# Norm factors of four batches: from scaled identities and products with ones to a store in DRAM and a broadcast read

## The chip, the cores and the metric

The kernel runs on one core of a Trainium2 chip. The metric is the device time of one execution in microseconds, the median of several. The engines are TensorE (PE, with its weight loads PEld), VectorE (DVE), ScalarE (ACT), GpSimd (POOL) and SyncE (SP, which here only issues DMAs). Each engine runs its own instructions in order.

## What is computed

Three layers follow each other on 4 x 576 = 2304 tokens of 512 features: a retention (attention with decaying causal weights, 8 heads), a gated unit behind an RMS norm, and a mixture of 8 experts with Sinkhorn-normalised weights. The change touches the norm at the start of the gated unit:

```python
rms = np.sqrt(np.mean(x * x, axis=-1, keepdims=True) + 1e-06)
xn = x / rms * rms_g
g = xn @ w_gate
silu = g * (1.0 / (1.0 + np.exp(-g)))
val = xn @ w_val
return (silu * val @ w_out).astype(np.float32)
```

`x` is the retention's output. 1/rms is one factor per token.

## The kernel before

Features lie on the 128 partitions, tokens in the free dimension: `acc_d[:, pr, tokens]` holds 128 of the 512 features. The program is written in the order in which each engine shall run it (a manual schedule); no planner moves anything.

**Retention.** 16 pairs of heads, pair i = batch b times 4 plus pr. In step i of the loop the code issues loads for pairs i+2 (q and v) and i+3 (k, twice), the scores of pair i+1 (`scores`, tile `sc`, then on VectorE the product with the mask, `am`), the states of pair i+1 (`states`), and the outputs of pair i (`outputs`, tile `o`, PSUM; VectorE multiplies it into `acc`, line 345). ScalarE squares the result (`sq`), GpSimd adds the squares of a batch's four pairs (line 352). `step_weights` puts one step of the preparation of the gated unit's weights (tiles `raw`, `cv`, `wslots`) into each pair. A pair's q has three buffers, k has two; all loads but the first are issued by SyncE, each when its buffer is free.

**The norm** of batch b is two generators that the loops push on, one step at a time.

- `norm_sums(b)`: products of the squares with ones put the tokens on the partitions (`ss`), a power of -0.5 on GpSimd (`ry`), and one pair later a Newton step on VectorE. The result `r` is 128 x 5: token c*128 + p lies at partition p, column c.
- `norm(b)`: the factors have to stand along the free dimension on all partitions. ScalarE scales an identity by each column of `r` (tile `dg`), TensorE multiplies it with ones (`rb`, `rbt`), ScalarE copies the result to `y`. Then follow four steps, one for each `pr`: VectorE scales `x` by `y` and the weight `rms_g` in place, ScalarE rounds it to `xhi`, and VectorE or GpSimd takes the rest, `xlo`, of the step before.

`SUMS_AT` places the sums of batches 0 to 2 at pairs 5 and 6, 9 and 10, 13 and 14; batch 3's follow in the first block of the gated unit. `norm(0)` starts with pair 7 and makes one step in each pair; `norm(1)` makes its first two steps in pairs 13 and 15:

```python
if i >= 2 * NP - 1:
    next(norms[0], None)
if i in (B * NP - 3, B * NP - 1):
    next(norms[1])
```

**The gated unit** runs over 5 blocks of tokens. A block multiplies its tokens with two gate and two value slices (`gv`, four times 12 products), forms the gated product (`t`, then `ghi` and `glo`), and multiplies it with two slices of the output weight (`x`). The first block begins when the retention has ended, and its first PSUM tile takes the bank of the last `o`. The norm of batch j+1 is made within block j.

Of the kernel before, what the change touches and what calls it, by code (L numbers as in the profile page):

```python
# [9 lines left out]
F32 = mybir.dt.float32  # L10
# [7 lines left out]
B, H, S, D = 4, 8, 576, 64  # L18
NP = H // 2
# [6 lines left out]
C = 128  # L26
NC = S // C
TAIL = S - NC * C
# [23 lines left out]
def retention_glu_experts(ctx: ExitStack, tc: tile.TileContext, a, out):  # L52
# [6 lines left out]
    nc = tc.nc  # L59
# [6 lines left out]
    kept = ctx.enter_context(tc.tile_pool(name="kept", bufs=1, space=bass.MemoryType.DRAM))  # L66
# [6 lines left out]
    ident = const.tile([128, 128], F32, name="ident")  # L73
    ones = const.tile([128, 128], F32, name="ones")
# [9 lines left out]
    def f32(t):  # L84
        return t.bitcast(F32)
# [13 lines left out]
    nrm = glu.enter_context(tc.tile_pool(name="nrm", bufs=1, side="right"))  # L99
# [3 lines left out]
    def load_weights(most=2):  # L103
        for _ in range(most):
            if n_load[0] == len(sources) or not raw_slots:
                return
            i = n_load[0]
            n = raw_of[i] = raw_slots.pop(0)
            t = rawp.tile([128, 1024], I32, tag=f"raw{n}", name=f"raw{i}")
            nc.sync.dma_start(t, sources[i].bitcast(I32))  # L110
            raw[i], asked[i] = t, n_step[0]
            n_load[0] += 1
# [37 lines left out]
    def step_weights(load=True, apart=2):  # L150
        for i in sorted(active):
            if next(active[i], True):
                del active[i]
        i = n_next[0]
        n_step[0] += 1
        if i in raw and len(active) < NCONV and n_step[0] - asked[i] > apart:
            active[i] = prepare(i)
            next(active[i])
            n_next[0] += 1
        if load:  # L160
            load_weights()
# [81 lines left out]
    psa = psa_pools.enter_context(tc.tile_pool(name="psa", bufs=2, space=PSUM))  # L243
# [15 lines left out]
    def load_pair(i, *names, queue=nc.sync):  # L259
        if i >= B * NP:  # L260
            return
        b, pr = divmod(i, NP)
        t = {}
        for n in names:
            t[n] = ld.tile([128, a[n].shape[-1]], F32, tag=n, name=f"{n}{i}", bufs=2 if n[0] == "k" else 3)
            queue.dma_start(t[n], a[n][b, pr])
        loaded.setdefault(i, {}).update(t)

    def scale_keys(i):
        if i >= B * NP:  # L270
            return
        for h in range(2):
            hh = 2 * (i % NP) + h
            ks = loaded[i]["ks"].rearrange("p (c h d) -> p c h d", h=2, d=D)[:, :, h, :]
            nc.scalar.mul(ks, ks, g_key[:, hh:hh + 1])
# [77 lines left out]
        squares[b] = sq  # L353
        yield

    normed, rstd = set(), {}

    def bank(name):
        pool, tag = ps_home
        return pool.tile([128, 512], F32, tag=tag, name=name)  # L360

    def two_banks(b):
        if b < 2:
            t = psa.tile([128, 2, 512], F32, tag="sc", name=f"rb{b}")
            return t[:, 0], t[:, 1]
        return bank(f"rb{b}"), bank(f"rbt{b}")

    def norm_sums(b):

        sq = squares.pop(b)  # L370
        if b < B - 1:
            ss = psa.tile([128, 2, 512], F32, tag="sc", name=f"ss{b}")[:, 0, :NC + 1]
        else:
            ss = bank(f"ss{b}")[:, :NC + 1]
        for c in range(NC + 1):
            w = C if c < NC else TAIL
            nc.tensor.matmul(ss[:w, c:c + 1], lhsT=sq[:, c * C:c * C + w], rhs=ones[:, :1], start=True, stop=True)
        v = nrm.tile([128, NC + 1], F32, tag="rv", name=f"rv{b}")
        r = nrm.tile([128, NC + 1], F32, tag=f"ry{b}", name=f"ry{b}")
        t = nrm.tile([128, NC + 1], F32, tag="rt", name=f"rt{b}")  # L380
        nc.vector.memset(v, 1.0)
        nc.vector.tensor_scalar(v[:, :NC], ss[:, :NC], 1.0 / DM, 1e-6, ALU.mult, ALU.add)
        nc.vector.tensor_scalar(v[:TAIL, NC:], ss[:TAIL, NC:NC + 1], 1.0 / DM, 1e-6, ALU.mult, ALU.add)
        nc.gpsimd.tensor_tensor(out=r, in0=v, in1=mhalf, op=ALU.pow)
        yield
        nc.vector.tensor_mul(t, r, r)
        nc.vector.scalar_tensor_tensor(t, t, -0.5, v, ALU.mult, ALU.mult)
        nc.vector.scalar_tensor_tensor(r, t, 1.5, r, ALU.add, ALU.mult)
        rstd[b] = r

    def norm(b):
        r = rstd.pop(b)
        dg = nrm.tile([128, (NC + 1) * C], F32, tag="dg", name=f"dg{b}")
        dg = dg.rearrange("p (c i) -> p c i", i=C)
        for c in range(NC + 1):
            nc.scalar.mul(dg[:, c, :], ident, r[:, c:c + 1])
        yield
        rb, rt = two_banks(b)
        rt = rt[:, :TAIL]
        nc.tensor.matmul(rb, lhsT=ones, rhs=dg[:, :NC, :], start=True, stop=True)  # L400
        nc.tensor.matmul(rt, lhsT=ones[:TAIL, :], rhs=dg[:TAIL, NC, :TAIL], start=True, stop=True)
        y = nrm.tile([128, (NC + 1) * C], F32, tag="dg", name=f"y{b}")[:, :S]
        nc.scalar.copy(y[:, :NC * C], rb)
        nc.scalar.copy(y[:, NC * C:], rt)
        yield
        ts = slice(b * S, (b + 1) * S)
        for pr in range(NP):
            x = acc_d[:, pr, ts]
            nc.vector.scalar_tensor_tensor(x, x, rms_g[:, pr:pr + 1], y, ALU.mult, ALU.mult)
            nc.scalar.copy(xhi[:, pr, ts], x)  # L410
            if pr:
                p = acc_d[:, pr - 1, ts], f32(xhi[:, pr - 1, ts])
                (nc.vector if pr % 2 else nc.gpsimd).tensor_sub(xlo[:, pr - 1, ts], *p)
            yield
        nc.vector.tensor_sub(xlo[:, pr, ts], acc_d[:, pr, ts], f32(xhi[:, pr, ts]))
        normed.add(b)

    ps_home = [psa, "o"]
    sums, norms = [norm_sums(b) for b in range(B)], [norm(b) for b in range(B)]
# [34 lines left out]
    for i in range(B * NP):  # L454
        b, pr = divmod(i, NP)
        load_pair(i + 2, "qT", "vs")
        load_weights(1)
        if i == 2:
            nc.sync.dma_start(rms_g, a["rms_g"])
            nc.sync.dma_start(ident, a["ident"])  # L460
            nc.sync.dma_start(wg[:, :KD * E], a["wg"])
        scores(i + 1)
        states(i + 1)
        load_pair(i + 3, "kT", "ks")
        scale_keys(i + 2)
        out_steps = outputs(i)
        next(out_steps)
        step_weights(load=False, apart=1)
        next(out_steps)
        if i in SUMS_AT:  # L470
            next(sums[i // NP - 1], None)
        if i >= 2 * NP - 1:
            next(norms[0], None)
        if i in (B * NP - 3, B * NP - 1):
            next(norms[1])
    assert 0 in normed
    retention.close()
# [145 lines left out]
    for s in range(NSWEEP):  # L623
        last_sweep = s == NSWEEP - 1
        for j, (t0, n) in enumerate(BLOCKS):
            last = j == len(BLOCKS) - 1
            block = gated_block(s, t0, n, last, pmm, pac, hp, tp, 1 if last_sweep and last else KD, 512)
            first_norms = not s and j + 1 < B
            assert s or (t0 + n - 1) // S in normed
            for i in range(2 * SWEEP + 1):  # L630
                if last_sweep and last and i == 2 * SWEEP:
                    break
                if first_norms and j and not i:
                    next(norms[j + 1])
                if i == 2 * SWEEP:
                    step_weights()
                next(block)
                if first_norms:
                    for _ in range((1, 1, 1, 2, 0)[i]):
                        next(norms[j + 1], None)  # L640
                    if not j and i in (1, 2):
                        next(sums[B - 1], None)
                    if i == 2 * SWEEP - 1 and j + 2 < B:
                        next(norms[j + 2])
                if i == 2 * SWEEP or i < 2 and not first_norms or i == 2 and not s:
                    step_weights()
                if last_sweep and j and i % 2:
                    next(scored)
                if last_sweep and j == 1 and i == 2:
                    load_job(0)  # L650
                    load_job2(0)
                if last_sweep and j >= 3:
                    next(first_unit, None)
                    if j == 4:
                        next(first_job, None)
            else:
                for _ in block:
                    assert 0
# [648 lines left out]
```

## Time and profile before

| | |
|---|---|
| median of 3 runs | 2000.43 us (1999.23 to 2001.38) |
| the profiled execution | 1999.34 us, its span 1997.6 us |
| TensorE busy | 1980.8 us, 99% of the span |
| VectorE, ScalarE, GpSimd busy | 72%, 44%, 37% |
| granted TensorE clock | 1.000 on average (2.4 GHz) |
| DMA | 436.56 MB, mean 219 GB/s |
| retention | about the first 85 us |

The page gives the busy time of each engine and a chain of waits. How the parts of the first 125 us hang together is read from the timelines of the engines: start, length, engine, line, operation, tiles, and in brackets for how long the engine had been idle and what ended that. A timeline merges equal instructions that follow each other ("x16").

### The profile page before, as it was taken

What the parts mean: (1) busy time and instruction counts of PE and PEld (TensorE: products, weight loads), DVE (VectorE), ACT (ScalarE), POOL (GpSimd) and SP (SyncE); (2) the same over time, 40 slices, a digit from 0 to 9 for tenths busy, and PEclk for the clock granted to TensorE, in tenths of its full rate; (3) what the DMA queues carried; (4) which work ended last, traced back from release to release, by engine and by line L of the source; (5) the groups of instructions that cost most, each with busy time, mean ns of one, the idle gap of its engine ahead of it and who ended that gap; (6) DMA issues with size and microseconds to landing.
All of it is one profiled execution on the core that took longest, in us unless ns stands there. A gap on an engine that the chain in (4) does not pass through costs nothing.

```text
span 1997.6 us, 29892 instructions
## 1 busy us (share of the span) xinstructions
PE 1980.8 (99%) x11390; PEld 1854.0 (93%) x11390; DVE 1442.0 (72%) x2275; ACT 869.0 (44%) x1649; POOL 744.1 (37%) x693
## 2 busy tenths in 40 slices
PE   9999999999999999999999999999999999999998
PEld 7788988988888999999999999999999999999998
DVE  7865555554688777777786777777787777777777
ACT  4453323322454544444444444444445444444443
POOL 3300000000154445455534544445466454444543
PEclk9999999999999999999999999999999999999999
DMA  9411111110188888888888676767767677676763
GB/s 318 147 32 53 53 42 53 43 43 1 48 308 304 289 296 309 306 299 308 299 314 314 247 277 237 278 247 270 262 241 282 258 262 275 239 267 248 275 257 143
DMA packets 111535, 436.56 MB, mean 219 GB/s; under 512 B 11720, under 2 KB 29128, under 8 KB 95008
## 3 DMA queue, kind: packets, MB, share of 16 engines
q1 hardware_dynamic: 109904, 432.39, 59.2%
q8 instruction: 89, 1.46, 0.3%
q10 hardware_dynamic: 1248, 1.49, 0.2%
q0 software_dynamic: 240, 0.79, 0.1%
q14 instruction: 54, 0.44, 0.1%
HBM read 312.41 MB, written 122.21 MB: 218 GB/s over the span
## 4 chain that ended last, share of the span: by engine, by line
PE 95%; DVE 3%; ACT 1%; DMA 1%; POOL 0%; issue 0%; ACTq 0%; DVEq 0%
PE pz L747 10%; PE py L747 10%; PE px L747 10%; PE qx L992 7%; PE qy L992 6%; PE qz L992 6%; PE gv L178 5%; PE gv L180 5%; PE gv L179 5%; PE y L179 4%; PE y L180 4%; PE y L178 4%; PE qz L747 3%; PE x L179 2%; PE x L178 2%; PE x L180 2%
## 5 line engine op out<-in xcount | busy, mean ns | idle before, releaser
L747 PE MATMUL py<-sx,w1s 128*128 128x384 f32 x1152 | 232.0, 336 | 0.8 <-ACT py L1084 0.6
L539 POOL TENSOR_TENSOR t<-rw 128x256 f32<-128x256 f32 x32 | 43.8, 1369 | 503.7 <-DVE sx L576 397.2
L1173 POOL TENSOR_TENSOR acc<-z,a_block 128x384 f32<-128x384 f32 x63 | 64.0, 1016 | 434.6 <-DVE z L1167 434.6
L747 PEld LDWEIGHTS py<-sx,w1s 128*128 128x128 f32 x1152 | 203.0, 188 | 4.9 <-ACT py L1084 1.9
L747 PE MATMUL px<-xhi,w1s 128*128 128x384 f32 x640 | 188.8, 335 | 1.0 <-DVE t L206 1.0
L982 ACT CAST xhi<-acc 128x384 fp32r<-128x384 f32 x316 | 156.0, 514 | 69.7 <-POOL acc L1173 35.5
L986 DVE TENSOR_TENSOR xlo<-acc,xhi 128x384 fp32r<-128x384 f32 x191 | 178.5, 961 | 1.8 <-ACT xhi L982 1.8
L986 POOL TENSOR_TENSOR xlo<-acc,xhi 128x384 fp32r<-128x384 f32 x125 | 148.6, 1189 | 26.3 <-ACT xhi L982 26.3
L1000 DVE TENSOR_TENSOR acc<-acc,qz 128x384 f32<-128x384 f32 x246 | 134.9, 548 | 25.2 <-PE qz L992 25.1
L206 DVE TENSOR_TENSOR t<-t,gv 128x512 f32<-128x512 f32 (+1 forms) x60 | 38.0, 634 | 123.5 <-PE gv L180 122.3
L747 PEld LDWEIGHTS px<-xhi,w1s 128*128 128x128 f32 x640 | 117.9, 188 | 1.5 <-DVE t L206 1.3
L1000 DVE TENSOR_TENSOR acc<-acc,qx 128x384 f32<-128x384 f32 x123 | 67.4, 548 | 71.2 <-PE qx L992 71.2
L747 PE MATMUL pz<-sx,w1s 128*128 128x384 f32 x576 | 115.4, 334 | 0.0
L747 PE MATMUL pz<-xhi,w1s 128*128 128x384 f32 x384 | 113.9, 337 | 0.8 <-DVE z L915 0.8
L792 DVE SCALAR_TENSOR_TENSOR acc<-y,prob,acc 128x512 f32<-128x512 f32 x144 | 101.4, 742 | 8.2 <-PE y L180 8.2
L747 PE MATMUL px<-xlo,w1s 128*128 128x384 f32 x320 | 107.0, 334 | 0.0
L1018 ACT COPY qz<-qy 128x384 f32<-128x384 f32 x127 | 58.8, 463 | 106.8 <-PE qy L992 101.0
L180 PE MATMUL y<-xlo,xhi 128*128 128x512 f32 x264 | 103.8, 393 | 0.0
L179 PE MATMUL y<-xlo,xhi 128*128 128x512 f32 x264 | 103.6, 393 | 0.0
L178 PE MATMUL y<-xlo,xhi 128*128 128x512 f32 x264 | 102.6, 389 | 0.0
L747 PEld LDWEIGHTS pz<-sx,w1s 128*128 128x128 f32 x576 | 101.3, 188 | 0.7
L1010 ACT COPY qy<-qx 128x384 f32<-128x384 f32 x127 | 58.8, 463 | 95.2 <-PE qx L992 89.4
(397 smaller groups left out, 5880.5 us busy)
## 6 DMA issues: line engine op xcount, KB each, us to landing
w1s<-w_kept SPq DMA_DIRECT2D x64, 1792.0 KB, 7.1
w_kept<-w1s SPq DMA_DIRECT2D x32, 1792.0 KB, 6.6
rw<-in_w_dram SPq DMA_DIRECT2D x64, 512.0 KB, 5.4
w_kept<-xlo SPq DMA_DIRECT2D x64, 512.0 KB, 3.7
w2s<-w_kept SPq DMA_DIRECT2D x32, 1024.0 KB, 6.9
w_extra<-w_kept SPq DMA_DIRECT2D x32, 768.0 KB, 7.5
w_kept<-xlo SPq DMA_DIRECT2D x44, 384.0 KB, 4.2
w2c<-w_kept SPq DMA_DIRECT2D x32, 512.0 KB, 7.8
```

Source lines behind the costliest of these rows:

```text
L178: nc.tensor.matmul(ps, lhsT=lh, rhs=rh, start=start, stop=False)
L179: nc.tensor.matmul(ps, lhsT=lh, rhs=rl, start=False, stop=False)
L180: nc.tensor.matmul(ps, lhsT=ll, rhs=rh, start=False, stop=stop)
L747: nc.tensor.matmul(ps, lhsT=l, rhs=r[:, k, :], start=start and k == 0 and i == 0, stop=k == 1 and i == 2, skip_group_check=True,)
L792: nc.vector.scalar_tensor_tensor(o, y_2, pe, o, ALU.mult, ALU.add)
L982: nc.scalar.copy(hi, x)
L986: (engine or nc.vector).tensor_sub(lo, x, f32(hi))
L992: nc.tensor.matmul(ps, lhsT=l, rhs=r, start=start and i == 0, stop=i == 2, skip_group_check=True)
L1000: nc.vector.tensor_add(dst, dst, ps)
L1010: nc.scalar.copy(y, x)
L1018: nc.scalar.copy(z, y)
L1173: nc.gpsimd.tensor_add(sums[0], z[:, 0, :], h_blocks[0])
```

## The change

`norm_sums` ends with a store of `r` to DRAM, written so that the 576 tokens of a batch lie one behind the other there. `norm` begins with a load that reads this row for all 128 partitions into `y`. Scaled identities, products with ones and copies, and the PSUM tiles for them (`two_banks`), are gone. `norm(0)` now starts with pair 9 (the load) and scales in pairs 10 to 13; before, it scaled in pairs 9 to 12. `norm(1)` makes its first step (the load) in pair 14, and its four scalings one step of block 0 later. Both new DMAs are issued by SyncE.

```diff
@@ -386,22 +382,11 @@
         nc.vector.tensor_mul(t, r, r)
         nc.vector.scalar_tensor_tensor(t, t, -0.5, v, ALU.mult, ALU.mult)
         nc.vector.scalar_tensor_tensor(r, t, 1.5, r, ALU.add, ALU.mult)
-        rstd[b] = r
+        nc.sync.dma_start(rstd_kept[b].rearrange("c p -> p c"), r)
 
     def norm(b):
-        r = rstd.pop(b)
-        dg = nrm.tile([128, (NC + 1) * C], F32, tag="dg", name=f"dg{b}")
-        dg = dg.rearrange("p (c i) -> p c i", i=C)
-        for c in range(NC + 1):
-            nc.scalar.mul(dg[:, c, :], ident, r[:, c:c + 1])
-        yield
-        rb, rt = two_banks(b)
-        rt = rt[:, :TAIL]
-        nc.tensor.matmul(rb, lhsT=ones, rhs=dg[:, :NC, :], start=True, stop=True)
-        nc.tensor.matmul(rt, lhsT=ones[:TAIL, :], rhs=dg[:TAIL, NC, :TAIL], start=True, stop=True)
-        y = nrm.tile([128, (NC + 1) * C], F32, tag="dg", name=f"y{b}")[:, :S]
-        nc.scalar.copy(y[:, :NC * C], rb)
-        nc.scalar.copy(y[:, NC * C:], rt)
+        y = nrm.tile([128, S], F32, tag="y", name=f"y{b}")
+        nc.sync.dma_start(y, rstd_kept[b].rearrange("c p -> (c p)")[:S].partition_broadcast(128))
         yield
         ts = slice(b * S, (b + 1) * S)
         for pr in range(NP):
@@ -469,9 +454,9 @@
         next(out_steps)
         if i in SUMS_AT:
             next(sums[i // NP - 1], None)
-        if i >= 2 * NP - 1:
+        if i >= 2 * NP + 1:
             next(norms[0], None)
-        if i in (B * NP - 3, B * NP - 1):
+        if i == B * NP - 2:
             next(norms[1])
     assert 0 in normed
     retention.close()
@@ -630,13 +615,11 @@
             for i in range(2 * SWEEP + 1):
                 if last_sweep and last and i == 2 * SWEEP:
                     break
-                if first_norms and j and not i:
-                    next(norms[j + 1])
                 if i == 2 * SWEEP:
                     step_weights()
                 next(block)
                 if first_norms:
-                    for _ in range((1, 1, 1, 2, 0)[i]):
+                    for _ in range(((1, 1, 1, 2, 0) if j else (0, 1, 1, 2, 1))[i]):
                         next(norms[j + 1], None)
                     if not j and i in (1, 2):
                         next(sums[B - 1], None)
```

Not shown: `two_banks` and the table `rstd` are removed, and `rstd_kept`, four DRAM tiles of 5 x 128, is added. On TensorE and ScalarE the change only takes instructions away or, for the rounding to `xhi`, puts them one pair or step later. On SyncE and VectorE it moves others past them. In the rows below a name's last number is the tile's number in its build.

SyncE, loads around the end of pair 6 and the start of pair 7. Before, the loads of k and q for pair 9:

```order
L266 DMA kT_618<-in_kT_dram 128x576
L266 DMA ks_620<-in_ks_dram 128x512
L266 DMA qT_654<-in_qT_dram 128x576
L266 DMA vs_656<-in_vs_dram 128x576
L266 DMA kT_683<-in_kT_dram 128x576
L266 DMA ks_685<-in_ks_dram 128x512
```

And now:

```order
L266 DMA kT_622<-in_kT_dram 128x576
L266 DMA ks_624<-in_ks_dram 128x512
L385 DMA rstd_kept_117<-ry_585 128x5x1
L266 DMA qT_659<-in_qT_dram 128x576
L266 DMA vs_661<-in_vs_dram 128x576
L266 DMA kT_688<-in_kT_dram 128x576
L266 DMA ks_690<-in_ks_dram 128x512
```

The store of batch 0's factors now stands ahead of q and v of pair 9. In the same way batch 1's store stands ahead of q and v of pair 13, behind k of pair 13; the loads of y stand behind k of pair 12 (batch 0) and behind batch 2's store (batch 1).

VectorE, from the output product of pair 10 to the mask product of pair 12 (`rt`, `ry` are the Newton step of batch 1). Before:

```order
L345 TENSOR_TENSOR acc<-o_906,g_out 128x512
L386 TENSOR_TENSOR rt_862<-ry_861 128x5
L387 SCALAR_TENSOR_TENSOR rt_862<-rt_862,rv_860 128x5
L388 SCALAR_TENSOR_TENSOR ry_861<-rt_862,ry_861 128x5
L409 SCALAR_TENSOR_TENSOR acc<-acc,rms_g,y_789 128x576
L413 TENSOR_TENSOR xlo<-acc,xhi 128x576
L294 TENSOR_TENSOR am_947<-sc_946,masks 128x1024
```

And now:

```order
L345 TENSOR_TENSOR acc<-o_899,g_out 128x512
L382 TENSOR_TENSOR rt_855<-ry_854 128x5
L383 SCALAR_TENSOR_TENSOR rt_855<-rt_855,rv_853 128x5
L384 SCALAR_TENSOR_TENSOR ry_854<-rt_855,ry_854 128x5
L394 SCALAR_TENSOR_TENSOR acc<-acc,rms_g,y_860 128x576
L294 TENSOR_TENSOR am_940<-sc_939,masks 128x1024
```

The first `xlo` has left this place; it stands one pair later, behind one scaling.

VectorE, from the norm's part in pair 13 to the end of pair 14 (`rt`, `ry`: batch 2). Before:

```order
L415 TENSOR_TENSOR xlo<-acc,xhi 128x576
L294 TENSOR_TENSOR am_1153<-sc_1152,masks 128x1024
L314 SCALAR_TENSOR_TENSOR block_states_116<-acc,u_1151 128x256
L315 SCALAR_TENSOR_TENSOR mt_1173<-u_1151,tables 128x64
L343 TENSOR_TENSOR acc<-u_1076,g_out 128x64
L133 SCALAR_TENSOR_TENSOR cv_997<-raw_873,cv_997 128x512
L345 TENSOR_TENSOR acc<-o_1176,g_out 128x512
L386 TENSOR_TENSOR rt_1139<-ry_1138 128x5
L387 SCALAR_TENSOR_TENSOR rt_1139<-rt_1139,rv_1137 128x5
L388 SCALAR_TENSOR_TENSOR ry_1138<-rt_1139,ry_1138 128x5
L343 TENSOR_TENSOR acc<-u_1151,g_out 128x64
```

And now:

```order
L394 SCALAR_TENSOR_TENSOR acc<-acc,rms_g,y_860 128x576
L398 TENSOR_TENSOR xlo<-acc,xhi 128x576
L294 TENSOR_TENSOR am_1142<-sc_1141,masks 128x1024
L314 SCALAR_TENSOR_TENSOR block_states_116<-acc,u_1140 128x256
L315 SCALAR_TENSOR_TENSOR mt_1162<-u_1140,tables 128x64
L343 TENSOR_TENSOR acc<-u_1069,g_out 128x64
L133 SCALAR_TENSOR_TENSOR cv_990<-raw_866,cv_990 128x512
L345 TENSOR_TENSOR acc<-o_1165,g_out 128x512
L382 TENSOR_TENSOR rt_1132<-ry_1131 128x5
L383 SCALAR_TENSOR_TENSOR rt_1132<-rt_1132,rv_1130 128x5
L384 SCALAR_TENSOR_TENSOR ry_1131<-rt_1132,ry_1131 128x5
L400 TENSOR_TENSOR xlo<-acc,xhi 128x576
```

The last scaling and the third `xlo` of batch 0 now stand in pair 13, and its last `xlo` (L415, now L400) at the end of pair 14.

## Rows read from the trace of the kernel before

**Rows 1.** The page, part 1: busy time of each engine.

```profile
PE 1980.8 (99%) x11390; PEld 1854.0 (93%) x11390; DVE 1442.0 (72%) x2275; ACT 869.0 (44%) x1649; POOL 744.1 (37%) x693
```

**Rows 2.** Timeline of TensorE, 44 to 90 us: start, length, instruction.

```profile
44.89 1.16 PE L290 MATMUL sc<-qT,kT 64*128 64x128 f32 x16
...
49.14 1.13 PE L400 MATMUL rb<-dg,ones 128*128 128x512 f32 x2
...
50.43 1.15 PE L290 MATMUL sc<-qT,kT 64*128 64x128 f32 x15
...
83.60 1.12 PE L400 MATMUL rb<-dg,ones 128*128 128x512 f32 x2
...
85.04 0.50 PE L178 MATMUL gv<-xhi,wslots 128*128 128x512 f32 x1
```

**Rows 3.** Timeline of TensorE, 84 to 130 us, end of blocks 0 and 1.

```profile
99.77 0.39 PE L180 MATMUL x<-ghi,wslots 128*128 128x512 f32 x1
...
100.92 0.50 PE L179 MATMUL x<-glo,wslots 128*128 128x512 f32 x1 [0.23 <-DVE glo L208]
101.26 0.40 PE L180 MATMUL x<-ghi,wslots 128*128 128x512 f32 x1
...
103.54 1.12 PE L400 MATMUL rb<-dg,ones 128*128 128x512 f32 x2
...
104.96 0.50 PE L178 MATMUL gv<-xhi,wslots 128*128 128x512 f32 x1
...
121.43 1.02 PE L400 MATMUL rb<-dg,ones 128*128 128x512 f32 x2
...
122.74 0.50 PE L178 MATMUL gv<-xhi,wslots 128*128 128x512 f32 x1
```

**Rows 4.** Timeline of VectorE, 34 to 90 us.

```profile
41.75 0.17 DVE L388 SCALAR_TENSOR_TENSOR ry<-rt,ry 128x5 f32<-128x5 f32 x1
...
57.07 1.23 DVE L294 TENSOR_TENSOR am<-sc,masks 128x1024 f32<-128x1024 f32 x1 [0.16 <-PE sc L290]
...
61.30 0.17 DVE L388 SCALAR_TENSOR_TENSOR ry<-rt,ry 128x5 f32<-128x5 f32 x1
...
62.11 1.97 DVE L413 TENSOR_TENSOR xlo<-acc,xhi 128x576 fp32r<-128x576 f32 x1
...
67.97 1.21 DVE L294 TENSOR_TENSOR am<-sc,masks 128x1024 f32<-128x1024 f32 x1
...
70.00 1.24 DVE L127 TENSOR_SCALAR cv<-cv 128x512 f32<-128x512 f32 x1
...
73.55 0.75 DVE L413 TENSOR_TENSOR xlo<-acc,xhi 128x576 fp32r<-128x576 f32 x1
...
76.25 0.42 DVE L127 TENSOR_SCALAR cv<-cv 128x512 f32<-128x512 f32 x1
...
84.31 0.68 DVE L345 TENSOR_TENSOR acc<-o,g_out 128x512 f32<-128x512 f32 x1
```

**Rows 5.** Loads of q: one issued in 38 to 40 us, one in 53.5 to 54.

```profile
L266 SPq DMA_DIRECT2D qT<-in_qT_dram x1: 328/328/328, 39.7 to 39.7; - x1
DMA to landing us min/median/max: 4.1/4.1/4.1
...
L266 SPq DMA_DIRECT2D qT<-in_qT_dram x1: 327/327/327, 53.8 to 53.8; - x1
DMA to landing us min/median/max: 3.2/3.2/3.2
```

**Rows 6.** The page, part 3: DMA queue, packets, MB, share of 16 engines.

```profile
q1 hardware_dynamic: 109904, 432.39, 59.2%
...
q10 hardware_dynamic: 1248, 1.49, 0.2%
```

**Rows 7.** Timeline of GpSimd, 50 to 130 us.

```profile
61.85 1.62 POOL L352 TENSOR_TENSOR sq<-sq,sq 128x576 f32<-128x576 f32 x1 [2.50 <-ACT sq L350]
...
69.56 1.41 POOL L413 TENSOR_TENSOR xlo<-acc,xhi 128x576 fp32r<-128x576 f32 x1
...
79.25 1.42 POOL L352 TENSOR_TENSOR sq<-sq,sq 128x576 f32<-128x576 f32 x1 [8.29 <-ACT sq L350]
```

More of the change, by code (lines that the diff above doesn't have):

```diff
@@ L354, in outputs @@
         yield
-    normed, rstd = set(), {}
+    normed = set()
     def bank(name):
@@ L360, in bank @@
         return pool.tile([128, 512], F32, tag=tag, name=name)
[L362 to L366, printed above, removed]
+    rstd_kept = [kept.tile([NC + 1, C], F32, tag=f"rstd{b}", name=f"rstd_kept{b}") for b in range(B)]
     def norm_sums(b):
```

## The prediction

> **What bounds the kernel now.** I read the page's engine totals first, then TensorE's timeline, then the timelines of the engines around each place that the diff touches. TensorE (PE) is busy for 99% of the span [rows 1], so a removed TensorE instruction counts in full wherever TensorE is the one that is waited for. The change acts only in the first 125 us, and there are three kinds of ground there.
>
> Up to 57 us TensorE runs the retention pairs without a gap: pair 9's scores start at 44.89, and before those of pair 10 stands the spreading of batch 0, from 49.14 to 50.43 [rows 2]. From the mask product am of pair 11 (57.07) to the last output product of pair 15 (84.31 + 0.68 = 84.99) [rows 4] VectorE (DVE) runs one instruction after the other, and TensorE waits for it. The first product of the gated stage starts at 85.04 [rows 2], just behind that last output product, whose PSUM bank it takes over. After that TensorE is the bound again, with one wait at 100.92 [rows 3].
>
> **What is removed.** Four times two products with ones on TensorE, and on ScalarE four times five scalings and two copies.
> - Batch 0: 50.43 - 49.14 = 1.3 us of TensorE [rows 2], on the path.
> - Batch 1: the products fill 83.60 to 85.0, but gv waits for VectorE until 84.99 anyway. Worth nothing by itself: VectorE's end decides.
> - Batch 2: 104.96 - 103.54 = 1.4 us; batch 3: 122.74 - 121.43 = 1.3 us [rows 3], both on the path, and nothing else ends there: in the new order the last xlo of batch 1 needs to be there only at the fourth k of the next block.
> - The wait at 100.92: from 99.77 to 101.26 three products took 1.49 us instead of 3 x 0.23 [rows 3], 0.8 lost, because VectorE came late with glo. The new block 0 has one 0.8 us scaling less ahead of it, so I count it as gained.
>
> The gated stage so gives 1.4 + 1.3 + 0.8 = **3.5 us**. ScalarE's share is worth nothing: it is busy for 44% of the span [rows 1] and nobody waits for it at these places once y comes from a load.
>
> **What is added on SyncE's queue.** The four stores wait for the last Newton step. In pair 6 that step ends at 41.75 + 0.17 = 41.92 [rows 4]. Queued behind the store, in order, is the load of q for pair 9, which was issued at 39.7 and landed 4.1 us later [rows 5], at 43.8, 1.1 us before TensorE used it at 44.89. It can now be issued at 41.92 + 0.08 for the semaphore + 0.33 for the store's issue + 0.07, that is at 42.4. For its landing I take 3.2 us, the fast one of [rows 5], since SyncE has then issued nothing for 2.5 us and the rings run empty.
>
> The store itself is the unknown: no row of before moves single 4-byte pieces. It writes a 128 x 5 tile transposed, 640 pieces, 40 for each of the 16 DMA engines, ahead of q on the same rings. From below, such a piece costs nothing, if bytes alone count. From above it costs what a packet of queue q1 costs on average, 59.2% x 16 x 1997.6 / 109904 = 172 ns at 3.9 KB: 6.9 us for 40. Queue q10, with 1.2 KB packets, has 0.2% x 16 x 1997.6 / 1248 = 51 ns [rows 6]; it is nearest in size, so I take 51 ns and 40 x 51 ns = 2.0 us.
>
> The Trainium skill speaks against this store (DMA: Bandwidth & Descriptors, section Rules for kernel authors): "Strided / non-contiguous last dim" becomes "one descriptor per element". Its fit in Anatomy of one DMA (2.0 us plus bytes over 436 GB/s, stated for the other kind of DMA) would make the 2.5 KB free on the ring; by that estimate the sum below would be 2.6 us lower, the third rival's time. No row of before can tell these two apart.
>
> q for pair 9 then lands at 42.4 + 3.2 + 2.0 = 47.6, and TensorE stands for 2.7 us at 44.89. Less the 1.3 us of batch 0, the pairs from 10 on come **1.4 us later**.
>
> Batch 1's store, in pair 10, does the same to q of pair 13: ready at 61.30 + 0.17 = 61.47 [rows 4], q issued at 61.9, landed at 67.1, its scores done 1.1 us later at 68.2. VectorE is by then 1.2 earlier (next part): it could start am of pair 13 at 67.97 - 1.2 = 66.8 [rows 4], so it waits 1.4 (both sides shift by the 1.4 above). In return the weight step at 70.00, which took 1.24 instead of 0.42 [rows 4] because GpSimd was running a subtraction from 69.56 [rows 7], comes late enough to miss it: -0.8. Together **+0.6**. Batches 2 and 3 have only weight loads and y behind their stores, which the next blocks take up. The y reads are as large as a q load and should land like one [rows 5]; each has 5 us or more, so they cost nothing. Were y of batch 0, issued at some 53, to need over 8 us, VectorE would wait for it at 62.
>
> **What moves on VectorE.** Each step of batch 0's norm goes one pair later, so one scaling (0.7, as from 61.4 to 62.11 [rows 4]) enters the VectorE-bound stretch from pair 9, where it had been free. The first xlo took 1.97 at 62.11, against 0.75 at 73.55 [rows 4], since GpSimd had started its sum of squares at 61.85 [rows 7] and the two exclude each other: who starts first runs, the other waits. In the new order no Newton step stands ahead of it in its pair and it starts before GpSimd: -1.2. Together **-0.5**.
>
> Two other steps, however, move to where GpSimd starts: the third xlo into pair 13, behind rv and a scaling; and the last one into pair 14, behind Newton, which pushes GpSimd's sum back into the weight steps of pair 15. At either place VectorE may have to wait through a sum of 1.42, the length of the one at 79.25 [rows 7]. Both hang on a tenth of a microsecond. Bounds: nothing and 2.8; I take one of them, **+1.4**.
>
> **The sum.** End of the retention: +1.4 + 0.6 - 0.5 + 1.4 = +2.9. Gated stage: -3.5. In all -0.6 us, and everything behind is TensorE-bound and passes it on. The profiled execution took 1999.3 us (span 1997.6), so 1998.7; the median of the runs shown, 2000.4, is 1.1 above that execution, so I predict **1999.8 us**. A measurement of this kernel can tell about 0.2%, 4.0 us, from no change. My forecast is no change.
>
> **Rivals.**
> 1. *The store clogs the rings* (slower). Mechanism: the 640 pieces go through one at a time, and q of pairs 9 and 13 stand behind them. At 172 ns a piece: TensorE stands 42.4 + 3.2 + 6.9 - 44.89 = 7.6 before pair 9, 6.3 net; q of pair 13 comes 4.9 later still, 5.5 net instead of 0.6. Retention +6.3 + 5.5 - 0.5 + 1.4 = +12.7, in all +9.2: 2009.6 us. Each nanosecond above 51 costs 2 x 40 ns, so it turns into "slower" (+4.0) from 51 + 4600/80 = 108 ns. For it: q1's mean. Against: q10's, and that the pieces are small.
> 2. *The whole gain arrives* (faster): pieces are free and neither GpSimd sum gets in the way. TensorE still stands 42.4 + 3.2 - 44.89 = 0.7; less 1.3 is -0.6; q of pair 13 lands at 65.1, in time; -0.6 - 0.5 - 3.5 = -4.6: 1995.8 us. For it: only bytes need to count. Against: both tenths must fall well.
> 3. *Pieces free, one sum in the way*: -4.6 + 1.4 = -3.2: 1997.2 us. This is the outcome by the cited fit.
> 4. *Both sums in the way, pieces at 51 ns*: -0.6 + 1.4 = +0.8: 2001.2 us.
>
> That the products go but nothing is gained is part of the forecast: batch 1's lie beside VectorE, and batch 0's are outweighed by SyncE's wait.
>
> **How the numbers follow.** Forecast 0.45, third rival 0.22, fourth 0.11: no change, 0.78 together. Second rival 0.11 (faster), first 0.11 (slower). The range from 1996.2 to 2003.8 reaches almost to the second rival and up to a price near 100 ns a piece.
>
> **What would show it.** TensorE: a wait for q before the scores of pair 9 (2.7 us; under 1 if pieces are free, over 5 for the first rival), and pair 13's scores late. VectorE: the first xlo at 0.75 instead of 1.97; a step of about 2 us in pair 13 (third xlo) or pair 15 (weight steps). The retention's last output product ends near 88, and the first gv product right behind it. In the gated stage no gap between x and gv. If q of pair 9 lands in time, or if VectorE waits for y, the reasoning is wrong.

## The result, and the profile after

The changed kernel takes **2022.07 us** (median of 4 runs, 2021.33 to 2023.6) beside 1999.83 us for the kernel before: a ratio of 1.0111, interval 1.0099 to 1.0124. It is slower by some 22 us, 1.1%; 1999.8 us, no change, was forecast. The profiled execution took 2021.33 us, its span 2019.6. Of two experiments below one execution each took far longer than the others, 6164.24 us with the factors turned on TensorE and 4188.62 us with 64 bytes to a piece, and as the second of these is the profiled one, only the landings of its stores are read from that profile.

The profile page's engine totals, against [rows 1]:

```profile
PE 1982.6 (98%) x11374; PEld 1856.7 (92%) x11374; DVE 1440.8 (71%) x2275; ACT 860.6 (43%) x1621; POOL 742.1 (37%) x693
```

TensorE has 16 instructions fewer and yet 1.8 us more of busy time. The rest of the 22 us must be standing. The view of waits, TensorE alone, from 0 to 200 us (engine, line, what it waited for: us in total, times, longest):

```profile
PE sc L290 <- DMA qT<-in_qT_dram: 20.2, 5, 9.3
PE gv L178 <- DVE acc L345: 2.8, 1, 2.8
PE x L178 <- ACT ghi L207: 1.6, 1, 1.6
```

Where they stand shows in TensorE's timeline (start, length, instruction, the idle time before it and what ended it), against [rows 2, 3]:

```profile
53.75 2.08 PE L290 MATMUL sc<-qT,kT 64*128 64x128 f32 x16 [9.30 <-DMA qT<-in_qT_dram]
...
60.26 1.16 PE L290 MATMUL sc<-qT,kT 64*128 64x128 f32 x16
...
83.48 2.08 PE L290 MATMUL sc<-qT,kT 64*128 64x128 f32 x16 [8.67 <-DMA qT<-in_qT_dram]
89.13 1.16 PE L290 MATMUL sc<-qT,kT 64*128 64x128 f32 x16
...
104.02 0.79 PE L178 MATMUL gv<-xhi,wslots 128*128 128x512 f32 x1 [2.83 <-DVE acc L345]
...
117.68 0.39 PE L178 MATMUL x<-ghi,wslots 128*128 128x512 f32 x1
...
123.95 0.39 PE L178 MATMUL gv<-xhi,wslots 128*128 128x512 f32 x1
...
139.67 0.50 PE L178 MATMUL x<-ghi,wslots 128*128 128x512 f32 x1 [1.63 <-ACT ghi L207]
...
144.51 0.48 PE L178 MATMUL gv<-xhi,wslots 128*128 128x512 f32 x1
```

Three rows of the kernel before that [rows 2, 3] leave out, from the same view: the scores of pairs 12 and 13, and the first product of block 0's second half.

```profile
60.12 1.16 PE L290 MATMUL sc<-qT,kT 64*128 64x128 f32 x16
...
64.37 1.16 PE L290 MATMUL sc<-qT,kT 64*128 64x128 f32 x16
...
97.28 0.39 PE L178 MATMUL x<-ghi,wslots 128*128 128x512 f32 x1
```

Set start against start, the two timelines say where the time went:

| start of | before | after | later by | what came in between |
|---|---|---|---|---|
| scores of pair 9 | 44.89 | 53.75 | 8.9 | wait for q, 9.3; until then the loop ran 0.5 earlier |
| scores of pair 10 | 50.43 | 60.26 | 9.8 | half clock +2.3, products for batch 0 gone -1.3 |
| scores of pair 13 | 64.37 | 83.48 | 19.1 | second wait for q, 8.7, and a small one |
| first gv, block 0 | 85.04 | 104.02 | 19.0 | half clock in pair 13 +1.4, products for batch 1 gone -1.4; TensorE stands 2.8 in both, in three waits before and in one after |
| first x, block 0 | 97.28 | 117.68 | 20.4 | half clock +1.4 |
| first gv, block 1 | 104.96 | 123.95 | 19.0 | products for batch 2 gone -1.4 |
| first gv, block 2 | 122.74 | 144.51 | 21.8 | y of batch 2 late and half clock +4.1, products for batch 3 gone -1.3 |
| end of the span | 1997.6 | 2019.6 | 22.0 | |

"Half clock" is read from a pair's or block's own length: pair 9 takes 60.26 - 53.75 = 6.5 us where an undisturbed pair takes 4.25 (60.12 to 64.37), pair 13 takes 5.65, and block 0's first half 13.66 instead of 12.24. Busy time and granted clock by stretch (window, length, the busy time of PE, PEld, DVE, ACT and POOL with instructions, PEclk, DMA share, GB/s):

```profile
53.70:57.70 4.00, 3.95 (x44) 3.49 (x46) 1.59 (x2) 1.25 (x3) 0.00 (x0) 0.50 0.93 339
83.40:87.00 3.60, 3.52 (x38) 3.15 (x40) 1.26 (x2) 0.00 (x0) 2.11 (x2) 0.55 1.02 394
104.00:107.00 3.00, 2.98 (x7) 2.40 (x8) 0.00 (x0) 0.70 (x2) 1.41 (x1) 0.50 1.00 25
141.00:145.00 4.00, 4.00 (x12) 3.14 (x11) 3.90 (x8) 2.48 (x5) 0.00 (x0) 0.57 0.41 116
```

After it has stood for 9.3, 8.7 and 2.8 us, TensorE goes on at a mean granted clock of 0.50 to 0.55: the lower of its two levels (1.2 of 2.4 GHz) for all or most of the stretch. These three stretches cost 2.3 + 1.4 + 1.4 us. The fourth row is another case: after the 1.6 us TensorE first goes on at full clock (1.00 from 139.6 to 141.0), and falls to 0.50 at some 141.2, while it is working, until 144.5. Why it falls only then is not shown.

**The store.** SyncE's timeline has the first one where the prediction put it, with q for pair 9 right behind:

```profile
41.44 0.38 SPq L385 DMA_DIRECT2D rstd_kept<-ry  x1
42.30 0.34 SPq L266 DMA_DIRECT2D qT<-in_qT_dram  x1
```

But it lands after 9.3 us. The DMA issues in the stretches of the four stores (out<-in, queue, count, KB, us from issue to landing); a read of y lies in the third:

```profile
rstd_kept<-ry SPq DMA_DIRECT2D x1, 2.5 KB, 9.3
...
rstd_kept<-ry SPq DMA_DIRECT2D x1, 2.5 KB, 10.3
...
y<-rstd_kept SPq DMA_DIRECT2D x1, 288.0 KB, 10.9
rstd_kept<-ry SPq DMA_DIRECT2D x1, 2.5 KB, 11.1
...
rstd_kept<-ry SPq DMA_DIRECT2D x1, 2.5 KB, 9.1
```

What the DMA engines moved meanwhile, in stretches of 42 to 44, 46 to 52 and 54 to 56 us:

```profile
DMA packets 680, 0.07 MB, mean 33 GB/s; under 512 B 658, under 2 KB 658, under 8 KB 679
...
DMA packets 92, 0.20 MB, mean 33 GB/s; under 512 B 5, under 2 KB 5, under 8 KB 92
...
DMA packets 411, 0.81 MB, mean 404 GB/s; under 512 B 46, under 2 KB 46, under 8 KB 411
```

This is the central reading. The 640 pieces are in the records within 2 us. Then, for six us, the loads behind them crawl at 33 GB/s. The store has landed at 41.44 + 9.3 = 50.7; from 50 to 52 us they still move 25 GB/s, from 52 to 54 177, and then 404. TensorE gets its q at 53.75, 3.0 us after the store's landing, which is about the 3.2 us that the prediction took for this load alone. So the pieces don't take long to be handed out; they take long to be finished, and what is behind them comes as if it had been issued only then.

### The profile page after: what moved, and what is told of

The parts are those of the page before. It is cut to its first block, busy times and chain, and to the rows that moved or that the text cites. A ratio compares the mean times of both kernels' runs of the same rounds, so it can differ in the third digit from the quotient of the medians.

```text
span 2019.6 us, 29850 instructions
## 1 busy us (share of the span) xinstructions
PE 1982.6 (98%) x11374; PEld 1856.7 (92%) x11374; DVE 1440.8 (71%) x2275; ACT 860.6 (43%) x1621; POOL 742.1 (37%) x693
## 4 chain that ended last, share of the span: by engine, by line
PE 92%; DVE 3%; DMA 2%; ACT 1%; POOL 0%; issue 0%; SPq 0%; ACTq 0%; DVEq 0%; POOLq 0%
PE py L730 10%; PE pz L730 10%; PE px L730 10%; PE qx L975 6%; PE qy L975 6%; PE qz L975 6%; PE gv L178 5%; PE gv L180 4%; PE gv L179 4%; PE y L179 4%; PE y L180 4%; PE y L178 4%; PE qz L730 3%; PE x L179 2%; PE x L180 2%; PE x L178 2%
## 5 line engine op out<-in xcount | busy, mean ns | idle before, releaser
L179 PE MATMUL y<-xlo,xhi 128*128 128x512 f32 x264 | 103.6, 393 | 0.0
```

Source lines behind the costliest of these rows:

```text
L179: nc.tensor.matmul(ps, lhsT=lh, rhs=rl, start=False, stop=False)
```

## The experiments

Theories after the result: the kernel's loss is the store's alone (against: the moves, or the removed cover); and the store's cost comes from the number of its pieces, from their order on SyncE's queue, or from their lying side by side in DRAM.

### No store at all

```diff
-        nc.sync.dma_start(rstd_kept[b].rearrange("c p -> p c"), r)
...
-        nc.sync.dma_start(y, rstd_kept[b].rearrange("c p -> (c p)")[:S].partition_broadcast(128))
+        nc.sync.dma_start(y, fixed.rearrange("c p -> (c p)")[:S].partition_broadcast(128))
```

> The changed kernel without the four stores: y is read, at the same places, from one DRAM row that holds ones and is written once in pair 2, so the factors 1/rms are left out. Store theories (the 4-byte pieces, by their number or by where they land): both waits for q (9.3 and 8.7 us) and the half clock behind them go, and the sum of the prediction without its store terms is left: -1.3 (batch 0's products) -0.5 (VectorE) +0 to 2.8 (GpSimd's sums) -3.5 (gated stage), 1994.6 to 1997.4 us. If the reads of y or the new order of the steps cost the time, it stays above 2010.

1998.19 us, ratio 0.9991 (0.9982 to 1.0001). The 22 us are gone with the store, and the time is within 0.2% of before, 0.8 above the expected stretch. Its waits of TensorE tell why the gain is small:

```profile
PE sc L290 <- DMA qT<-in_qT_dram: 3.3, 6, 0.7
PE gv L178 <- DVE acc L345: 3.3, 1, 3.3
```

The second row is a new wait of 3.3 us at the seam to the gated stage, taken up again below.

### The store alone, in the kernel before

```diff
+        nc.sync.dma_start(rstd_kept[b].rearrange("c p -> p c"), r)
         rstd[b] = r
```

> The kernel before, with the four transposed stores added at the same places and read by nobody. Store theories: nearly the whole loss comes with them, two waits for q of some 9 us and 1 to 2 us of half clock behind each, 2018 to 2024 us; the loads of y are not there to wait. If the loss needs the reads of y or the new order, about 2000.

2020.59 us, ratio 1.0104 (1.0088 to 1.0119). The stores land after 9.4 to 11.5 us, and TensorE waits 21.4 us for q:

```profile
PE sc L290 <- DMA qT<-in_qT_dram: 21.4, 4, 9.7
```

The store makes nearly the whole loss with nothing else changed.

### The same 640 pieces, apart

Where a diff below names spread, rows or one, y reads the fixed row as above, and only the store's target differs.

```diff
+    spread = [kept.tile([NC + 1, C, 128], F32, tag=f"spread{b}", name=f"spread{b}") for b in range(B)]
...
+        nc.sync.dma_start(spread[b][:, :, 0].rearrange("c p -> p c"), r)
```

> As the kernel without stores, but with r stored, 640 pieces of 4 bytes, each into a 512-byte stretch of DRAM of its own (and never read). If the pieces cost by their number, on the rings or at the DRAM, the waits for q stay: 2016 to 2024 us. If they cost because they land beside each other and wait for one another, nearly all of it goes and SyncE's wait for Newton alone is left, 0.7 to 2 us before pair 9: 1996 to 2000.

1998.96 us, ratio 0.9998 (0.9989 to 1.0007). The group of its stores on SyncE's queue:

```profile
L386 SPq DMA_DIRECT2D spread<-ry x4: 370/377/378, 41.9 to 100.5; - x4
...
DMA to landing us min/median/max: 2.2/2.4/2.5
```

As many pieces of the same size (696 packets under 512 bytes from 41 to 46 us, 673 in the changed kernel), on the same queue, in the same order: 2.4 us instead of 9 to 11. So neither the number of the pieces nor the queue makes the loss by itself. Where they land does.

### Rows of 20 bytes

```diff
+    rows = [kept.tile([128, NC + 1], F32, tag=f"rows{b}", name=f"rows{b}") for b in range(B)]
...
+        nc.sync.dma_start(rows[b], r)
```

> As the kernel without stores, but with r stored as it lies, 128 rows of 20 bytes (and never read). By number of pieces: a fifth, so the waits for q fall from 9 to some 2 to 3 us and the clock holds: 1998 to 2003 us. By bytes landing beside each other: the same 2.5 KB, but a fifth of the writes, also 1998 to 2003. If SyncE's wait for Newton, and not the pieces, holds q back, it stays at 2015 to 2022.

2000.68 us, ratio 1.0002 (0.9992 to 1.0011); its stores land after 1.4 to 3.1 us. The same bytes lie side by side, but in 128 pieces. The number of pieces and their neighbours both had it there, so it doesn't tell these two apart; SyncE's wait for the Newton step, the third in the expectation, makes no loss.

### On ScalarE's queue

```diff
-        nc.sync.dma_start(rstd_kept[b].rearrange("c p -> p c"), r)
+        nc.scalar.dma_start(rstd_kept[b].rearrange("c p -> p c"), r)
```

> The changed kernel with its four transposed stores issued on ScalarE's queue in place of SyncE's. If the loads wait only because they stand behind the store on SyncE's queue, they now pass it: landings of 3 to 5 us, waits for q under 6 us in all, 1998 to 2002 us. If the writes of 4 bytes side by side hold the engines or the memory for everybody, the q load of pair 9 is still late by 5 us or more, and the time is 2010 to 2022 us.

2008.61 us, ratio 1.004 (1.0024 to 1.0055): between the two expectations, a miss for both. The q load of pair 9 isn't late here: SyncE issues it at 40.98, and ScalarE the store only at 43.22. The longest wait, 5.4 us, stands before the scores of pair 10. The waits, and the DMA issues of 38 to 48 us:

```profile
PE sc L290 <- DMA qT<-in_qT_dram: 10.1, 6, 5.4
```

```profile
kT<-in_kT_dram SPq DMA_DIRECT2D x3, 288.0 KB, 8.1
...
ks<-in_ks_dram SPq DMA_DIRECT2D x2, 256.0 KB, 11.0
rstd_kept<-ry ACTq DMA_DIRECT2D x1, 2.5 KB, 12.2
```

Loads on SyncE's own queue land after 8 to 11 us although no store stands in it; in the kernel before, k and ks take 4.2 us in the same stretch. Of the 20.2 us of waits for q 10.1 are left, and 3.3 with no store at all. So a part of the wait comes from the order on the queue, and a part reaches other queues. Whether it is held in the DMA engines or at the memory no run tells; that wasn't tried.

### How far apart, and how many

Four runs more: 64, 32 and 16 bytes to a piece (16, 8 and 4 in place of the 128 floats above), and one column alone, dense.

```diff
+        nc.sync.dma_start(one[b].rearrange("c p -> p c"), r[:, :1])
```

> As the run with each piece in its own 512 bytes (factors are stored but never read; y reads a fixed row of ones), but each of the 640 pieces has its own 64 bytes, eight pieces to each 512. If the unit in which neighbours disturb each other is 64 bytes or less, it is as fast as with 512: landings of 2 to 3 us, 1997.5 to 2000.5 us. If it is larger, landings are between 3 and 10 us and the time is 2003 to 2022 us.

> As the run with 64 bytes to a piece (factors stored but never read, y from a fixed row of ones), with 16 bytes to a piece, so that four pieces share 64 bytes where the changed kernel has 16. Theory A, writes into the same 64 bytes go one after another and different 64 bytes side by side: a landing of 9.3 us for 16 makes 2.3 us for 4, at most 4 us; time 1999 to 2004 us. Theory B, every 4-byte write that shares its 64 bytes costs the same in one common line (9.3 us / 640 = 14.5 ns each): landing 8 to 11 us, time 2012 to 2022 us.

> The transposed store cut to one of its five columns: 128 pieces of 4 bytes side by side in 512 bytes, 16 to each 64 bytes as in the changed kernel, but a fifth as many. Four fifths of the factors aren't stored and none is read; y reads a fixed row of ones. Theory A (by the neighbours in 64 bytes): landing 8 to 11 us as in the changed kernel, time 2012 to 2022 us. Theory B (by the number of pieces, 128 x 14.5 ns = 1.9 us): landing 2 to 3 us, time 1998 to 2002 us.

> As the runs with 64 and with 16 bytes to a piece (factors stored but never read, y from a fixed row of ones), with 32 bytes to a piece. Landings were 2.4 us with 64 bytes and 3.3 with 16, so the unit that neighbours share is above 16 bytes and at most 64. If it is 32 bytes, no piece has a neighbour here: landings of 2.2 to 2.5 us. If it is 64 bytes, two pieces share one: between 2.4 and 3.3, some 2.6 to 2.9 us. Either way the time is 1998 to 2002 us.

Landings of the one dense column, and of 16 and 32 bytes to a piece:

```profile
L386 SPq DMA_DIRECT2D one<-ry x4: 319/326/327, 42.6 to 116.9; - x4
...
DMA to landing us min/median/max: 8.0/8.0/8.1
```

```profile
L386 SPq DMA_DIRECT2D spread<-ry x4: 371/378/383, 42.2 to 104.6; - x4
...
DMA to landing us min/median/max: 3.1/3.3/3.6
```

```profile
L386 SPq DMA_DIRECT2D spread<-ry x4: 370/377/382, 43.1 to 102.2; - x4
...
DMA to landing us min/median/max: 2.4/2.7/3.2
```

| pieces | bytes to a piece | in each 64 bytes | landing, us | time, us | ratio (interval) |
|---|---|---|---|---|---|
| 640 | 512 | 1 | 2.2 to 2.5 | 1998.96 | 0.9998 (0.9989 to 1.0007) |
| 640 | 64 | 1 | 2.2 to 2.5 | 2001.28 | 1.0010 (1.0001 to 1.0019) |
| 640 | 32 | 2 | 2.4 to 3.2 | 1999.94 | 0.9999 (0.9988 to 1.0011) |
| 640 | 16 | 4 | 3.1 to 3.6 | 2002.65 | 1.0014 (1.0005 to 1.0023) |
| 128 | 4 | 16 | 8.0 to 8.1 | 2016.27 | 1.0082 (1.0067 to 1.0098) |
| 640 | 4, the change | 16 | 9.1 to 11.1 | 2022.07 | 1.0111 (1.0099 to 1.0124) |

The landings with 64 bytes were taken while the loads beside them went at half the rate (134 GB/s from 60 to 90 us, against 267 in the first 85 us of the kernel before), so that row weighs less than the others. The run with 64 bytes came out 0.8 us above what was expected of it, the one with 16 and the one column as theory A had it, the one with 32 as for a unit of 64. The two that tell the theories apart are 640 pieces at 16 bytes and 128 pieces at 4: the fewer pieces, in a fifth of the bytes, land 4.7 us later. By number it would be the other way. What counts is how many pieces share a short stretch of DRAM: counted by 64 bytes, (3.3 - 2.4) / 3 = 0.3 to (8.0 - 2.4) / 15 = 0.4 us for each further piece. That the stretch has 64 bytes and not 32 is what the landing at 32 bytes speaks for (2.7, between its neighbours), but it overlaps both, so it isn't settled. Nor is a longer stretch excluded: counted by 512 bytes, the same landings give (3.3 - 2.4) / 31 = 0.03 to (8.0 - 2.4) / 127 = 0.04 us a piece, which would put 64 bytes to a piece only some 0.2 us above 512.

### The factors turned on TensorE

With 512-byte rows to write, the change can be had as it was meant.

```diff
-        nc.sync.dma_start(rstd_kept[b].rearrange("c p -> p c"), r)
+        yield
...
+        nc.tensor.transpose(rt[:NC + 1, :], r, ident)
+        rs = nrm.tile([NC + 1, C], F32, tag="rs", name=f"rs{b}")
+        nc.scalar.copy(rs, rt[:NC + 1, :])
+        nc.sync.dma_start(rstd_kept[b], rs)
```

> The changed kernel with the factors turned on TensorE first: a third step of norm_sums, one pair later, transposes r into PSUM, ScalarE copies it out, and the store writes five rows of 512 bytes. Nothing is left out. If 4-byte writes side by side are the whole loss, it comes out near the kernel without stores: landings of the stores of 1.5 to 3 us, waits for q of 3 to 6 us, 1997.5 to 2000.5 us. If the transposition costs a wait of its own (its PSUM buffer is one of two that the scores take turns in, and SyncE now waits for ScalarE's copy), 2000.5 to 2004 us, with PE standing at sc for am or at q. If any store on that queue is what costs, 2010 us and more.

1999.31 us, ratio 0.9994 (0.9985 to 1.0003): the loss is gone, but no gain shows. The profile has no landing for these stores; q of pair 10, issued 0.4 us behind the first of them, lands after 3.5 us, and the waits for q are 2.9 us in all. VectorE's timeline at the seam to the gated stage:

```profile
84.63 1.88 DVE L133 SCALAR_TENSOR_TENSOR cv<-raw,cv 128x512 int32<-128x512 int32 x1
86.44 0.68 DVE L345 TENSOR_TENSOR acc<-o,g_out 128x512 f32<-128x512 f32 x1
```

The last copy of outputs (L345), for which the first gv product waits 2.88 us, stands behind a step of the weights that was made to wait through a sum of GpSimd's from 84.07 to 85.96 (1.88 instead of 0.67).

### The last copy first

```diff
+        if i == B * NP - 1:
+            next(out_steps)
         step_weights(load=False, apart=1)
-        next(out_steps)
+        if i < B * NP - 1:
+            next(out_steps)
```

> The kernel that turns the factors on TensorE, and for the last pair the copy of its outputs goes ahead of the step of the weights on VectorE (in the run before, PE waited 2.88 us there: the copy at 86.44 stood behind a 1.88 us step of the weights, and the products after it went at 0.63 us). Nothing is left out. If the removed products of batch 1 had covered this wait, and their gain was lost in it, the wait falls to about 1 us, the products stay at 0.39 us, and the time is 1996 to 1998 us, below the kernel before. If the step of the weights put back makes the first products late in its turn, PE waits for wslots instead and the time stays at 1998.5 to 2000.5 us.

**1995.23 us**, ratio 0.9979 (0.997 to 0.9988): faster than both kernels, by 4.4 us (0.2%) against before, and 0.8 below the expected stretch. TensorE's timeline:

```profile
84.61 0.50 PE L178 MATMUL gv<-xhi,wslots 128*128 128x512 f32 x1 [0.62 <-DVE acc L345]
...
97.92 0.27 PE L390 MATMUL rt<-ident,ry 128*5 128x128 f32 x1 [0.90 <-DVE ry L384]
97.95 0.48 PE L178 MATMUL x<-ghi,wslots 128*128 128x512 f32 x1
...
103.49 0.39 PE L178 MATMUL gv<-xhi,wslots 128*128 128x512 f32 x1
...
119.81 0.39 PE L178 MATMUL gv<-xhi,wslots 128*128 128x512 f32 x1
```

Against 85.04, 97.28, 104.96 and 122.74 before, that is -0.4, +0.7, -1.5 and -2.9. Block 0's first half takes 1.1 us longer: TensorE stands 0.90 for the Newton step of batch 3 before it turns these factors (L390). Its second half gains 2.1 us, the 1.4 of the products and the wait for glo; but glo is in time there because of the stand just before, so that nothing is left of the 0.8. Block 1 gains 1.5. The profiled execution is, at 1997.98 us, the slowest of the eleven and ends only 1.4 us ahead of the profile before; where it lost the rest behind block 1 is not shown.

### The last copy first, in the kernel before

The same edit of order, alone.

> The kernel before with the one edit of order: for the last pair the copy of its outputs goes ahead of the step of the weights. If the gain of the run before belongs to the change of the norm and was only uncovered by the order, the order alone is worth nothing here, since the copy at 84.31 was hidden behind the products for rb from 83.60 to 85.04: 1998.8 to 2000.8 us. If the order alone is the gain, 1995 to 1997.5 us.

2000.19 us, ratio 1.0002 (0.9993 to 1.0011). The order is worth nothing there. So the gain belongs to the change of the norm, with its removed products, and the order only uncovers it.

## Why the prediction was wrong

**The step that failed** is the price of the store: "I take 51 ns and 40 x 51 ns = 2.0 us". Its method was at fault, not only its size. It looked for a price per piece, from below nothing and from above 172 ns, and took the sum of prices as the landing. The stores land after 9.1 to 11.1 us. In the terms of the sum, TensorE gets q of pair 9 53.75 - 42.30 = 11.45 us after its issue, 8.25 above the 3.2 for the load alone where 2.0 was taken: 8.25 / 40 = 206 ns a piece, beyond the upper bound. And with the pieces apart all 640 land after 2.4 us, so it isn't a price per piece. The upper bound came from packets of 3.9 KB, which say nothing of 4-byte writes side by side, so it bounded nothing here. TensorE therefore stood 9.3 us where 2.7 was forecast, and 8.7 before pair 13 where the term was +0.6 in all. The first rival had the place and the sign (q of pairs 9 and 13, over 5 us), with a tenth of the chance, and by its price 2009.6, less than half of the loss; pieces "one at a time" was its mechanism, which the run with the pieces apart refutes.

On the Trainium skill (DMA: Bandwidth & Descriptors): the rule of one descriptor per element (Rules for kernel authors) agrees with the trace, 658 small packets from 42 to 44 us, just behind the store's issue, where 640 elements are stored. The fit of 2.0 us plus bytes (Anatomy of one DMA), stated there for the other kind of DMA, comes near the pieces apart, 2.4 us, and not those side by side, 9.3. The Trainium skill's Specifications on the same page say that below 512 bytes the engine reads, modifies and writes; pieces with 512 or 64 bytes to themselves land after 2.4 us here, so smallness alone isn't the price. A reading and rewriting of shared bytes would explain that neighbours wait for each other; no run shows it.

**Two steps more failed behind it.**
- "so they cost nothing", of the y reads: y of batch 2, issued at 122.75 behind batch 3's store (118.72) and a load of 512 KB, landed after 9.6 us, and VectorE stood for it (the DMA issues of that stretch, then VectorE's timeline):

```profile
y<-rstd_kept SPq DMA_DIRECT2D x1, 288.0 KB, 9.6
```

```profile
132.40 0.82 DVE L394 SCALAR_TENSOR_TENSOR acc<-acc,rms_g,y 128x576 f32<-128x576 f32 x1 [6.78 <-DMA y<-rstd_kept]
```

  That is the wait at 139.67 and, with the half clock in the same block, 4.1 us. With no stores VectorE waits 0.2 us for y, with the turned factors 1.6 to 1.7, and no such delay reaches TensorE.
- No term had TensorE's clock in it. Half clock cost 5.1 us behind the first three stands, and about 1.5 of the 4.1 in block 1 (products 0.43 us apart instead of 0.23).

**What held.** The place: the loads of q behind the stores. That q of pair 9 is issued at 42.30 where 42.4 was forecast is partly luck: from the end of the Newton step (41.24 + 0.17) to its issue it took 0.9 us, not the 0.5 of the sum, but the loop ran 0.5 us earlier. The products of batch 2 are worth the 1.4 us; those of batches 0 and 3 can't be told from the clock's part in the changed kernel and are taken at their length before, 1.3 each. Of GpSimd's two sums exactly one is in the way, as in the sum: the first xlo takes 0.75; the third one 0.74, and the sum beside it waits (2.09 instead of 1.42); the step of the weights in pair 15 is the one that waits through the other (1.88 instead of 0.67), as the timelines of VectorE and GpSimd show:

```profile
76.19 0.75 DVE L398 TENSOR_TENSOR xlo<-acc,xhi 128x576 fp32r<-128x576 f32 x1
...
95.71 0.74 DVE L398 TENSOR_TENSOR xlo<-acc,xhi 128x576 fp32r<-128x576 f32 x1
...
101.48 1.88 DVE L133 SCALAR_TENSOR_TENSOR cv<-raw,cv 128x512 int32<-128x512 int32 x1
```

```profile
95.63 2.09 POOL L352 TENSOR_TENSOR sq<-sq,sq 128x576 f32<-128x576 f32 x1 [10.12 <-ACT sq L350]
...
100.92 1.89 POOL L352 TENSOR_TENSOR sq<-sq,sq 128x576 f32<-128x576 f32 x1 [2.06 <-ACT sq L350]
```

**What was priced at nothing and is not.** Batch 1's products are indeed hidden, as forecast, but they also kept TensorE busy up to the first gv product [rows 2]. With them gone it stands 2.8 us for L345, and in the changed kernel goes on at half clock.

**A gain that was counted and didn't come.** The 0.8 at the wait for glo: in the changed kernel 0.23 before L179 is still there (121.32). The scaling that left block 0 doesn't stand in glo's way: VectorE, on its way to glo, sits idle for 1.08 us until GpSimd has made `ry` of batch 3, before (96.50) and after (116.91). With the factors turned the wait for glo is gone, with either order of the last copy, but TensorE then stands 0.90 for the same Newton step instead.

## What to carry to other kernels

A store is priced by where its pieces land and not only by their number and size: before writing a tile transposed, four bytes at a time, turn it on chip or leave room between the pieces, and look at the landing, since whatever is queued behind waits for that. A cost without a near row in the trace needs a bound by mechanism; the dearest row at hand isn't one. And work that is hidden may itself be the cover of a wait: ask what stands bare when it goes.

## What the runs showed of the hardware

- 4-byte writes side by side in DRAM: 128 of them (512 bytes) land after 8.0 us, 640 after 9.1 to 11.1; 640 with 64 or 512 bytes to each after 2.4. The same 2.5 KB as rows of 20 bytes, a little over three to 64 bytes, land after 1.4 to 3.1, in the middle 1.7.
- Such a store slows loads of another queue too: 8 to 11 us to landing with the store on ScalarE's queue, 4.2 in the same stretch of the kernel before, and 10.1 us of waits for q instead of 20.2.
- While it lands, the DMA engines' records move 33 GB/s (46 to 52 us); from 54 to 56 us 404.
- In the changed kernel TensorE, after it had stood for 2.8 to 9.3 us, went on at the lower level of its clock (0.50 to 0.55); after 1.6 us it went on at full clock and fell 1.5 us later, at work.
